# Ten more DMA transposes, issued from ScalarE's queue as well as SyncE's, with three smaller edits, in a fused linear-attention and MLP kernel

One Trainium2 chip, one core. The metric is device time in microseconds (us) of the core, median of several executions; lower is better. The kernel before takes 165.2 us. "Fast" and "slow" are two states in which executions of one kernel fall: a run that is over 1.5% longer than the fastest run of the same kernel is called slow, and only fast runs are compared.

## The reference

```python
def _attn_ref(q, k, v, alpha):                 # B, H, S, D = 4, 8, 768, 48, float32
    state = zeros((B, H, D, D))
    for t in range(S):
        state = alpha[:, :, t, :, None] * state + einsum('bhd,bhe->bhde', k[:, :, t], v[:, :, t])
        y[:, :, t] = einsum('bhd,bhde->bhe', q[:, :, t], state)
    return y

def _moe_ref(x, U, V, w_ch1, w_ch2):           # x: (4, 768, 384), the heads of y side by side
    h = x.transpose(0, 2, 1) @ U @ V           # U: (768, 32), V: (32, 768): low rank over time
    u = x + h.transpose(0, 2, 1)
    return u + maximum(u @ w_ch1, 0.0) @ w_ch2 # w_ch1: (384, 1536), w_ch2: (1536, 384)
```

The kernel cuts the 768 time steps of each of the four batches (0 to 3) into six chunks of 128. A chunk needs cumulated logarithms of alpha, k and q scaled by their exponentials (`rk`, `rq`), both transposed (`kt`, `qt`), scores, a causal mask (`pm`) and a running state (`st`). When a batch is complete, its x goes through the low-rank product (`utx`, then h), u = x + h, and two layers: MLP1 (`uT` times `w_ch1`, relu to `h1t`) and MLP2 (`h1t` times `w_ch2`, added to u). MLP1 needs u transposed: this is `uT`.

## The kernel before

The program calls `P.add` once for every operation; a long table then gives the order. A number in it is one `P.add`, and a letter behind it chooses the engine where there is a choice (A ScalarE, V VectorE, G GpSimd, S SyncE). Every engine works through its own operations in the order of the table. The table was made for this very program, so any edit of the operations needs a new one.

```python
PAIR = (0, 1)
TRD = {(3, c) for c in range(2, NC)}   # chunks whose k and q are transposed by DMA
TRU = (3,)                             # batches whose u is transposed by DMA
XT = (0, 1)                            # batches whose x is transposed, and h added in PSUM
# ... cut ...
# a chunk's decay totals: a zero or a large negative number (offd) is put under them by a
# matmul, then one activation
nc.tensor.matmul(cb()[:, DM : DM + 2 * HP], lhsT=ident, rhs=offd.rearrange("p a b -> p (a b)"), start=False, stop=False)
for p in range(HP):
    nc.tensor.matmul(cb()[:, DM + 2 * p : DM + 2 * p + 2], lhsT=lt()[:, 2 * p : 2 * p + 2, :].rearrange("t h w -> t (h w)"),
                     rhs=ones, start=False, stop=(p == HP - 1))
# ... cut ...
P.add({"ACT": 100}, lambda e: nc.scalar.activation(tot()[:, :, 0], cb()[:, DM : DM + 2 * HP], AF.Exp), r=[cb], w=[tot])
# ... cut: k and q of a chunk ...
if (b, c) in TRD:
    for ring, dst in ((rk, kT), (rq, qT)):
        P.add({"SP": 1250.0}, lambda e, ring=ring, dst=dst: nc.sync.dma_start(dst(), ring().rearrange("t h w -> t (h w)"), transpose=True),
              r=[ring], w=[dst], mode="X")
else:
    tk, tq = Buf(bank), Buf(bank)      # transposes on TensorE, then copies out of PSUM
# ... cut: u of a batch that is not in XT, chunk by chunk ...
P.add({"DVE": 465}, lambda e, c=c, hb=hb: nc.vector.tensor_tensor(ub()[:, c, :], xb()[:, c, :], hb()[:, 0:DM], op=ALU.add), ...)
if b in TRU:
    P.add({"SP": 1250.0}, lambda e, c=c: nc.sync.dma_start(uT()[:, :, c * C : (c + 1) * C], ub()[:, c, :], transpose=True),
          r=[(ub, c)], w=[(uT, c)], mode="X")
```

## Time and profile before

| | before |
|---|---|
| time, fast runs | 165.2 us (164.81 to 165.96) |
| span of the profiled run | 162.8 us |
| first MLP1 matmul | 29.4 us |
| end of the last matmul | 159.5 us |
| DMA transposes | 14, all issued by SyncE |

A profiled time in the views below is counted from the start of the span; the time of a run is some 2 us more than its span. The lines on which the reading rests stand in the prediction. To read a line of a group: source line, engine, operation, output and inputs, count, busy time and mean; in the chain of what ended last: start, length, what.

### The profile page before, as it was taken

How to read it: one execution, taken by the hardware profiler on the slowest of the kernel's cores; microseconds unless marked ns; L12 is line 12 of the kernel's file. 1: busy time of each engine (PE TensorE's matmuls, PEld its weight loads, DVE VectorE, ACT ScalarE, POOL GpSimd, SP SyncE). 2: the span in 40 equal slices, each digit the busy share in tenths (PEclk: the TensorE clock that was granted, in tenths of full speed). 3: DMA queues.
4: the chain of work that ended last, by engine and by line, in shares of the span. 5: the costliest groups of instructions: out<-in, count | busy, mean ns of one | idle time of the engine just before them, and what ended most of it. 6: DMA issues, size and time to landing. Idle time of an engine off the chain costs nothing.

```text
span 162.8 us, 4450 instructions
## 1 busy us (share of the span) xinstructions
PE 154.6 (95%) x1691; PEld 102.8 (63%) x1691; DVE 111.1 (68%) x240; ACT 87.9 (54%) x214; POOL 66.2 (41%) x106
## 2 busy tenths in 40 slices
PE   7878789999999999999999999999999999999991
PEld 2536677666666877766666766766667566666660
DVE  6389997536756989765579677896689465562512
ACT  4747787848594797956944557655432201330300
POOL 3228866659318625173685533519533000000000
PEclk9999999999999999999999999999999999999998
DMA  5999999999999999997998995995757133402124
GB/s 132 268 262 264 258 273 290 345 246 290 347 237 245 233 199 222 172 200 132 240 192 184 226 238 125 194 170 105 99 115 242 52 71 74 144 1 101 48 84 158
DMA packets 89876, 30.43 MB, mean 187 GB/s; under 512 B 83680, under 2 KB 89824, under 8 KB 89856
## 3 DMA queue, kind: packets, MB, share of 16 engines
q1 hardware_dynamic: 89856, 30.16, 81.7%
q8 instruction: 13, 0.21, 0.6%
q14 instruction: 7, 0.06, 0.1%
HBM read 23.79 MB, written 4.72 MB: 175 GB/s over the span
## 4 chain that ended last, share of the span: by engine, by line
PE 86%; DVE 6%; DMA 3%; SPq 2%; issue 1%
PE ps L798 29%; PE ps L773 29%; DMA io<-in_k_dram 3%; PE ps L435 3%; PE ps L543 2%; DVE pm L473 2%; SPq L356 2%; PE ps L604 2%; PE ps L625 2%; DVE rq L422 2%; PE ps L684 1%; PE ps L718 1%; PE ps L494 1%; PE ps L462 1%; PE ps L566 1%
## 5 line engine op out<-in xcount | busy, mean ns | idle before, releaser
L798 PE MATMUL ps<-w_sb,h1t 128*128 128x384 bf16 x288 | 54.2, 326 | 0.0
L773 PE MATMUL ps<-uT,w_sb 128*128 128x384 bf16 x288 | 50.9, 326 | 0.0
L783 ACT ACTIVATE h1t<-ps 128x384 bf16<-128x384 f32 x46 | 21.4, 496 | 35.4 <-PE ps L773 35.1
L785 DVE TENSOR_SCALAR h1t<-ps 128x384 bf16<-128x384 f32 x50 | 25.8, 552 | 21.0 <-PE ps L773 20.9
L773 PEld LDWEIGHTS <-w_sb 128*128 128x128 bf16 x288 | 27.3, 98 | 16.6
L798 PEld LDWEIGHTS <-h1t 128*128 128x128 bf16 x288 | 26.4, 97 | 16.4 <-issue 0.6
L635 DVE TENSOR_TENSOR pm<-ps,maskc 128x512 bf16<-128x512 f32 x24 | 15.6, 684 | 2.6 <-PE ps L625 2.5
L473 DVE TENSOR_TENSOR pm<-ps,maskp 128x512 bf16<-128x512 f32 x24 | 15.8, 682 | 1.3 <-PE ps L462 1.3
L584 POOL TENSOR_TENSOR rk<-io,ai 128x384 bf16<-128x384 f32 x12 | 11.0, 915 | 10.0 <-PE ps L773 3.9
L584 POOL TENSOR_TENSOR rq<-io,aa 128x384 bf16<-128x384 f32 x12 | 11.0, 927 | 2.2 <-ACT aa L578 1.2
L807 DVE TENSOR_TENSOR ou<-ub,ps 128x384 f32<-128x384 bf16 x12 | 6.4, 552 | 7.3 <-PE ps L798 7.1
L313 ACT CAST xb<-ps 128x384 bf16<-128x384 f32 x15 | 7.3, 491 | 7.0 <-PE ps L684 5.4
L317 POOL CAST rw<-io 64x384 bf16<-64x384 f32 x14 | 7.0, 503 | 8.0 <-DMA io<-in_v_dram 7.2
L317 POOL CAST rv<-io 128x384 bf16<-128x384 f32 x12 | 6.0, 503 | 9.6 <-DMA io<-in_v_dram 9.6
L317 POOL CAST w_sb<-io 128x384 bf16<-128x384 f32 x16 | 7.7, 507 | 4.7 <-DMA io<-in_moe_w_ch_dram 4.7
L313 ACT COPY kt<-ps 128x512 bf16<-128x512 bf16 x13 | 8.0, 612 | 2.5 <-PE ps L435 2.0
L313 ACT COPY qt<-ps 128x512 bf16<-128x512 bf16 x11 | 7.4, 677 | 3.3 <-PE ps L435 1.7
L315 DVE COPY qt<-ps 128x512 bf16<-128x512 bf16 x9 | 5.6, 627 | 4.6 <-PE ps L435 3.5
L659 POOL TENSOR_TENSOR st<-sm,tot 128x384 bf16<-128x384 f32 x6 | 5.0, 831 | 9.1 <-DVE sm L671 9.1
L422 POOL TENSOR_TENSOR rk<-io,ai 128x384 bf16<-128x384 f32 x8 | 7.3, 912 | 3.3 <-DMA io<-in_k_dram 1.4
L422 POOL TENSOR_TENSOR rq<-io,aa 128x384 bf16<-128x384 f32 x7 | 6.4, 913 | 5.3 <-ACT aa L416 5.3
L731 DVE TENSOR_TENSOR ub<-xb,ps 128x384 bf16<-128x384 bf16 x12 | 6.0, 550 | 3.3 <-PE ps L730 3.3
(120 smaller groups left out, 262.1 us busy)
## 6 DMA issues: line engine op xcount, KB each, us to landing
io<-in_q_dram SPq DMA_DIRECT2D x24, 192.0 KB, 4.4
...
```

What stands on the lines that cost most here:

```text
L313: nc.scalar.copy(dst, src)
L317: nc.gpsimd.tensor_copy(dst, src)
L422: eng.tensor_tensor(jh(dst()[:, :, 0:D]), raw(a), jh(x()), op=ALU.mult)
L473: nc.vector.tensor_tensor(dst, s2, maskp.to_broadcast([C, 2, 2, C]), op=ALU.mult)
L584: eng.tensor_tensor(dst()[:, :, 0:D], a(), x(), op=ALU.mult)
L635: nc.vector.tensor_tensor(pm()[:, :, par, :], s2, maskc.to_broadcast([C, HP, C]), op=ALU.mult)
L731: P.add({"DVE": 465}, lambda e, c=c, hb=hb: nc.vector.tensor_tensor(ub()[:, c, :], xb()[:, c, :], hb()[:, 0:DM], op=ALU.add), r=[hb] + xk( ...
L773: nc.tensor.matmul(hb()[:, 0:TW], lhsT=w1_sb[:, ct, jt * 128 : (jt + 1) * 128], rhs=uT()[:, ct, tt * TW : (tt + 1) * TW], start=(ct == 0), ...
L783: nc.scalar.activation(dst, hb()[:, 0:TW], AF.Relu)
L785: nc.vector.tensor_scalar_max(dst, hb()[:, 0:TW], 0.0)
L798: nc.tensor.matmul(hb()[:, 0:DM], lhsT=h1()[:, jt, c * C : (c + 1) * C], rhs=w2_sb[:, jt, :], start=(jt == 0), stop=(jt == NJ - 1 and not ...
L807: P.add({"DVE": 468}, lambda e: nc.vector.tensor_tensor(ou(), (xb if b in XT else ub)()[:, c, :], hb()[:, 0:DM], op=ALU.add), r=[hb] + (xk ...
```

## The change

The intent is to take work from TensorE, which is busy without a gap from 29.4 us on. The four parts, and the core of the diff (the order table is new as a whole and left out; `Plan.place`, which fits buffers to expected times, gets a case for transposes on ScalarE). A fifth part goes with the table: the diff also lets more operations choose their engine, and the new table uses it. Of the 24 scalings that make `rk` and `rq` of batches 2 and 3, all on GpSimd before, six now stand on VectorE, five of them for batch 3.

```diff
-    TRD = {(3, c) for c in range(2, NC)}
-    TRU = (3,)
-    XT = (0, 1)
+    TRD = {(3, c) for c in range(NC)}     # 4 more transposes of k and q by DMA
+    TRU = (2, 3)                          # 6 more transposes of u by DMA
+    XT = (0,)                             # batch 1's u as the sum x + h on VectorE
...
+    def queue(eng):
+        return nc.scalar if eng == "ACT" else nc.sync
...
-                    {"SP": 1250.0},
-                    lambda e, ring=ring, dst=dst: nc.sync.dma_start(dst(), ring().rearrange("t h w -> t (h w)"), transpose=True),
+                    {"ACT": 1250.0, "SP": 1250.0},
+                    lambda e, ring=ring, dst=dst: queue(e).dma_start(dst(), ring().rearrange("t h w -> t (h w)"), transpose=True),
... the same for the transpose of u ...
-            nc.tensor.matmul(cb()[:, DM : DM + 2 * HP], lhsT=ident, rhs=offd.rearrange("p a b -> p (a b)"), start=False, stop=False)
+        def f_tot(e):                     # the offset comes as the bias of two activations
+            for i in range(2):
+                nc.scalar.activation(tot()[:, i : 2 * HP : 2, 0], cb()[:, DM : DM + HP], AF.Exp, bias=offb[:, i : i + 1])
... MLP2: chunk 5 of batch 3 in two column parts, each with its add and its store ...
+        parts = [(0, 256), (256, DM)] if b == B - 1 and c == NC - 1 else [(0, DM)]
```

In the new table 19 of the 24 transposes are on ScalarE's queue and five on SyncE's (q of chunks 2 and 4 of batch 3; u1, u3 and u4 of batch 3). Where one queue's transposes follow the other's, the later ones must wait for the earlier ones to land.

More of the change, by code (lines that the diff above doesn't have):

```diff
@@ L118, in place @@
                 end[op] = dma + 850.0
+            elif eng == "ACT" and op.mode == "X":
+                dma = max(dma, t) + 500.0
+                clock[eng] = t + cost
+                end[op] = t + 2650.0
             elif eng == "SP":
@@ L153 @@
 TABLE = """
-67 65 69 179 61 182 201 184 157 77 62 63 183 66 204 160 205 187G 247 189 161 162 207 64 68 191V 164V 166 186V 188 190A 185 168V 165V 73 71 167 192 70
-181G 180G 224 206 163 159G 169V 81 74 170 194 172 193 75 158G 209G 3 78 79 76 82 72 195 250 227 196 208V 83 173 211 210 251 228 268 229 197 213A 2 231G
-171 174 80 271 175 198 212V 214 273 274 272 84 85 176 89 232V 233 253 252 234 215 254G 6 5 199 177 255G 4 226G 275G 203G 15 31 33 35 236V 23 13 17 93
-19 21 27 29 235A 237 43 25 87 86 1 97 39 90 216 200A 238 256 257 230 225A 259A 258V 240 202A 178A 241 239 242 260 277 276V 243 244 217 249G 218 270G
@@ L158 @@
-219 88 95 278 37 41 262 261 51 47 49 91 279A 245 220 280A 222 248A 94 269G 8 281 7 57 59 45 55 221 388 263 283 53 101 96 32 34 16 36 264 18 14 24 20 92
-284 285 98 105 391 410 394 246A 107 103 99 100 102 265 266 413 392 393 22 28 30 26 286 282 287 9 11 395G 0 267V 223V 288A 289 290 295 10V 12A 291A 414
-292 304 298 299 293 296 300A 396G 301 417G 302 305 297A 307 308 294V 306V 303V 309A 415 332 330 328 352 354 331A 329A 432 416 336 355V 353A 435 356 438
-357A 333V 344 312 340 320 314 345A 315A 313A 436 346 310 338 342 321V 455 337V 437 109 106 343V 112 104 108 113 316 398 334 318 347V 341V 335V 339V
@@ L162 @@
-311A 44A 40A 400A 390A 440G 38G 42G 348 458 397 419 326 322 317V 323V 349V 399A 327A 401 319A 461 389G 460 459 403 418V 421V 48G 439G 383 404 358 442
-324 325A 50A 402 405 406 368 46G 420 350 412G 52A 444A 58A 441 411G 434G 433G 462G 407G 351V 422V 443A 363 364 359 56A 54A 60A 478 423 445 384 369 370
-424 446 425 481 360 499 482 483 426 448 486G 447 361 371 449 502 385 365 505 450V 504 453 507G 427 386 428 366 509 464 488 485G 429G 511V 463V 110 362
-111 129 367 457A 503 456A 490A 454A 408 471 378 409A 619 466A 451 506V 465 430 487 508 117 379 133 467V 472 123 116 121 114 118 115 473G 468 119 120
@@ L166 @@
-122 489V 130 125 431A 484 510A 479A 480A 500A 131 127 124 387 136 474 135 126 128 137 149 491 512 470 452V 493 492 469 373 494 380 475G 501A 638 621
-374 495 640 515 623 622 496G 513 516 514 476 625 517V 375 497 627 381 629V 477A 626 620 642 641 376 718 498A 624 518 628 630V 720 519A 529 520 521 631
-722 721 723 658 522V 535 523 526 633 833 527 538 539 524 530 528A 525V 660 536 532 533 531A 537V 634 662 540A 661 663 545 561 551 635 534V 587 559 644
-664 645 639 585 588V 560A 581 546A 557 541 659 562A 643 569 567 632 553 570A 678 558A 542V 552V 554V 582A 372 134 666 575 680 145 573 681 682 574A 568A
@@ L170 @@
-683 586A 563 141 132 139 564A 668A 665 685 684 583 576V 584V 543 653 636 835 544A 646 837 647 547 555 649V 648A 637A 565 549 673 654 556V 548V 687 550A
-836 667 144 377 655G 679 674 686 589 571 590 688V 566V 669V 572V 725 675G 724 838 698 689A 690 650 670 671 651 652 699 591 700 579 702 703 701 852 580V
-592 692 705 704 609 656 594 595 727 693 577 691 657V 729A 672 694 578V 596 726 593 706 707 696 604 695V 597 697A 839 605 606 841 708A 709A 728A 713 714
-614 843A 138 730 710 732 712 872 890 676 610 840 719 715G 854 731 677V 711 611 612 607 857 855 599 733 842 892 856 908 734A 844A 834 858 859 874 716
@@ L174 @@
-615 717V 845 875 893 735 600 861 877 142 143 598 613 153 140 147 148 154 895 736A 894 150 146 876 863A 926 847 846 751 745 743 860 749 616 744 746 752
-853 878 750 739 740 848 601 879 753 747 737 850 849 617 862A 738 754A 864 151 155 867 928 741 851V 866 748A 783 910 781 782A 929 742V 784V 868 931 911
-773 797 865 602 880 798A 777 779 799 800A 912 913 785 765 930 786V 778V 780V 766V 870 757 932 891 896 871V 881 898 761 795 791 771 775 758A 772A 796V
-792V 787 873 897 915 933 914 869G 759 801 767 789 774A 768A 760A 776V 802V 885 899 917 763 769 788V 790V 886 916 887G 764A 770A 755 903 152 882 762V
@@ L178 @@
-909 900 918 756A 884 901 935 902 919 904 808 809 934 818 803 793 883 810 921 888 794A 156 905V 920 922 936 906 924 804 805 937 938 907A 923G 618 603
-608 382 927 939 940A 889V 925V 806 813 941 942A 828 946 807 958 819 943 949 947 950 959 829 955 820 814 952 948 815 823 824 944 825 956 951 945 953 826
-816 821 811 954 960 957 830 969 965 817 822 967 963 961 977 968A 966V 971 983 984A 964A 962V 981 972V 978V 985 1005 831 991 975 1014 973 976V 1009 970V
-987 1006A 992V 974A 986A 988V 982V 1010 979 980A 832 995 989 990V 996A 1011 1007 993 999 1015 1016 1001 997 1012 1002V 994V 1000V 1017 1019 1003 1034
@@ L182 @@
-1013 1020 812 1018 1021 1022 1029 1024 998A 1008A 1004A 1025 1026 1035 1030 1036 1027 1023 1028 827 1031 1037 1038 1032 1033
+61 73 69 62 68 63 224 157 160 227 163 161 201 162 65 1 164G 3 180G 4 165G 179 0 204 166 182 167 67 71 66 64 205 206 183 184 187V 169A 189 186G 77 70 81
+75 74 72 191V 188 78 168A 207 158G 159G 79 190V 209V 181A 228 185 230 76 82 170 192 195 173 247 229 208G 232G 171 194 231G 193 268 174 196 83 80 84 89
+250 211 85 6 210 172 5 212A 271 15 17 33 13 202G 234 175 197 176 198 213A 236A 251 214 233 199 216 203G 274 252 253 200A 272 254V 217 255G 218 256 258A
@@ new lines @@
+226A 273 225G 235V 275G 237 177 219 215 276G 220 257 240 238 221 239 27 25 29 86 31 241 21 19 259A 23 93 87 222 2 249G 242 269G 8 178A 277 260 7G 243
+223A 278 248A 245 279V 18G 280A 263 270A 410 264 281 261 262 265 244 282 388 266 16G 246A 14G 284 285 283 35 97 90 413 37 88 39 49 391 267A 286 43 94
+51 45 30G 28G 41 91 47 95 53 287 57 96 9 11 288A 289 12V 10A 290 298 292 295 301 22G 291A 392 293 299 296 300V 307 302 308 294A 92 99 59 304 297A 309A
+303A 305 306A 34A 26A 314 310 312 311A 336 338 313A 337A 348 322 350 334 349V 315V 339V 335V 323A 416 346 324 432 415 414 393 24G 20G 435 320 342 344
@@ new lines @@
+55 101 325A 347V 343V 345V 32G 396G 395G 389G 40G 36A 351A 321A 318 398 352 356 340 436 353A 438 397 319A 357V 399V 417V 341V 354 328 316 332 400A 329V
+419 355V 44G 439G 455 394 326 390A 38G 42G 418G 105 98 107 100 401 103 52A 437 421V 317V 403 402 404 441 333V 458 460 46A 461 50A 330 48G 363 443A 383
+368 364 420 58A 459 331A 405 406 440V 442 106 369 102 384 444A 434A 412G 407G 60A 56A 327V 422V 423 445 478 499 425 358 447 424 446 359 54G 411G 408
+426 409V 427 428 385 433G 463G 448 481 449 462V 450V 502 365 483 451 482 484 504 452V 386 507V 360 465 108 104 361 366 109 110 113 111 486G 453 370
@@ new lines @@
+467A 454A 503 367 112 129 362 117 488 430 114 121 131 118 116 485V 506V 464 487 509 508 371 466V 457A 431A 489A 511A 505 510V 490V 378 456G 429G 471
+119 122 120 133 115 123 130 125 468 512 472 480G 473G 479A 491 379 470 469 492 474 513 618 501A 500A 373 494 380 475G 515 495 476 620 493 516 496G 374
+514 497 517G 518 637 621 622 624G 477V 498V 623 519A 625V 375 619A 520 376 381 521A 627 626 633 629V 522 524 528 523 126 127 124 639 530 525 137 536
+628A 717 382 529 372 128 134 141 630 641 657 642 526 531 632 527A 640 532 534 135 659 719 533V 634 631 537 542 558 540 662 677 721 660 559A 552 679 535
@@ new lines @@
+553A 724G 643G 638A 722 538 554 645 541V 539V 647V 145 132 138 143 139 387 720 681 680 682 555A 661 562 563V 664G 683G 572 560 570 564 582 574 571V
+543V 561V 663G 568 566 652 583A 832 575A 565A 569A 834 584 666 685 653 573V 837 668A 835 836 658A 136 665 580 586 644G 684G 550 667A 687V 567V 581V
+585V 654G 686 149 150 144 377 140 672 646 548 551A 549A 673 674G 723G 678G 648V 635 688V 546 544 697 556 547V 587A 636A 545V 649 669 689 699 557V 700
+849 702 650 670 671 691 690 651 593 588 589 692 590 726 725 701 727V 591 693 703G 675 851 695 705 578 707V 728V 576 704G 706 694G 853 698A 579A 854 867
@@ new lines @@
+577A 852 696V 708V 838V 712 608 603 676V 713 729 709 840A 711 730 731 710 609 869 594 595 655 839G 841A 714G 718G 732 885 871 870 656A 715 872 733A 887
+610 596 855V 716V 734 874G 856G 735V 611 833G 592 146 151 612 155 147 153 842 604 142 154 148 745 605 598 857A 889 858A 888 890 843 746 844 850G 747A
+845 748 751 742 736 749 846 752 750A 753A 599 847 600 859 739 743 903 737 860 861 876S 613 614 615 865 862 905 848V 606 863 601 866V 740 784 792 778
+790 780 785V 781V 786 782 616 783V 793V 738A 907 906 800 798 788 796 909G 864G 779V 789V 868G 891G 892G 787V 910V 912S 152 744A 741A 766 776 768 607
@@ new lines @@
+156 791A 908 911A 762 921 894A 767V 873V 769V 801V 923 777A 925 924 886G 928G 760 772 763V 761V 794 754 880 756 926 893A 875A 795V 773V 774 881 882G
+930A 898 755V 797V 775V 899 927V 770 817 764 758 818 799A 771A 757V 759A 877 895 879 878 896 765A 897 913 802 929A 803 804 807 904G 900G 915 914 916
+901 917 918G 931 922G 933 932 919 808 827 883 934 597 935A 902A 809 828 920V 884V 936 937A 812 938 805 810 939 944 822 941 813 829 947 945 942 806 602
+617 943S 948 830 823 950 951 949S 952S 811 940A 946A 953 819 824 814 820 954 966 960 962 956 961A 967A 964 974 965V 957V 975V 825 970 968 958 972 955A
@@ L183 @@
+990 986 826 831 821 973V 969V 984 959V 987A 991A 994 1000 1002 963V 1003V 985V 1014 980 988 992 993V 1001V 981A 982 971A 983V 815 1009 1010 996 978 976
+979A 997V 977V 998 1015 999V 995A 1016 1004 1017 989V 1005 1006 1019 1020 1029 1021 1018 816 1007 1011 1008 1024 1022 1012 1032 1033 1030 1013 1025
+1023 1034 1026 1031 1027 1028
 """
@@ L254 @@
     ut_ones, upto, below = tri[:, 0, :], blocks[:, 0, :], blocks[:, 1, :]
-    ones = const.tile([C, 2], BF16, name="ones")
+    ones = const.tile([C, 1], BF16, name="ones")
     nc.vector.memset(ones, 1.0)
+    offb = const.tile([C, 2], FP32, name="offb")
+    nc.vector.memset(offb, 0.0)
+    nc.vector.memset(offb[0:64, 1:2], -30000.0)
+    nc.vector.memset(offb[64:128, 0:1], -30000.0)
     onesel = const.tile([C, 2, 2], BF16, name="onesel")
@@ L321, in small @@
         P.add({"SP": 500.0}, lambda e: nc.sync.dma_start(v_in, moe_V), w=["v_in"])
-        P.add({"POOL": 300}, lambda e: nc.gpsimd.tensor_copy(u_sb, u_in), r=["u_in"], w=["u"])
+        P.add({"POOL": 300, "ACT": 280}, lambda e: copy(e, u_sb, u_in), r=["u_in"], w=["u"])
         P.add({"POOL": 800}, lambda e: nc.gpsimd.tensor_copy(v_bf, v_in), r=["v_in"], w=["v_bf"])
@@ L341, in weights1 @@
             for ct in range(NCT):
-                weight(w1_sb[:, ct, cs], moe_w_ch1[ct * 128 : (ct + 1) * 128, cs], ("w1", g, ct), {"POOL": 485})
+                weight(w1_sb[:, ct, cs], moe_w_ch1[ct * 128 : (ct + 1) * 128, cs], ("w1", g, ct), {"POOL": 485, "ACT": 435})
     def weights2():
@@ L403, in f_cum @@
             nc.tensor.matmul(cb()[:, Q : 2 * Q], lhsT=upto, rhs=l2[:, 1], start=False, stop=False)
-            nc.tensor.matmul(cb()[:, DM : DM + 8], lhsT=ident, rhs=offd.rearrange("p a b -> p (a b)"), start=False, stop=False)
-            tot4 = cb()[:, DM : DM + 8].rearrange("p (c a b) -> p c a b", c=2, a=2)
+            nb = 2 if b == 0 else 1
+            if b == 0:
+                nc.tensor.matmul(cb()[:, DM : DM + 8], lhsT=ident, rhs=offd.rearrange("p a b -> p (a b)"), start=False, stop=False)
+            tot4 = cb()[:, DM : DM + 4 * nb].rearrange("p (c a b) -> p c a b", c=2, a=2)
             for a in range(2):
@@ L409, in f_cum @@
                         tot4[:, :, a, :], lhsT=lt()[:, HP * j + 2 * a : HP * j + 2 * a + 2, :].rearrange("t h w -> t (h w)"),
-                        rhs=onesel, start=False, stop=(a == 1 and j == 1),
+                        rhs=onesel[:, :, 0:nb], start=False, stop=(a == 1 and j == 1),
                     )
-        P.add({"PE": mm(DM, Q, Q, 8, 4, 4, 4, 4)}, f_cum, r=[lt], w=[cb])
+        P.add({"PE": mm(DM, Q, Q, 4, 4, 4, 4, *([8] if b == 0 else []))}, f_cum, r=[lt], w=[cb])
         aa, ai, tot = Buf(aas), Buf(ais), Buf(tots)
@@ L416, in stage_pair @@
         P.add({"ACT": 390}, lambda e: nc.scalar.activation(aa().rearrange("t h d -> t (h d)"), cb()[:, 0:DM], AF.Exp), r=[cb], w=[aa])
-        P.add({"ACT": 100}, lambda e: nc.scalar.activation(tot()[:, :, 0], cb()[:, DM : DM + 8], AF.Exp), r=[cb], w=[tot])
+        def f_tot(e):
+            if b == 0:
+                nc.scalar.activation(tot()[:, :, 0], cb()[:, DM : DM + 8], AF.Exp)
+                return
+            for i in range(2):
+                nc.scalar.activation(tot()[:, i : 2 * HP : 2, 0], cb()[:, DM : DM + HP], AF.Exp, bias=offb[:, i : i + 1])
+        P.add({"ACT": 100 if b == 0 else 200}, f_tot, r=[cb], w=[tot])
         rq, rk = Buf(rqs), Buf(rks)
@@ L560, in stage_gla @@
         rv = Buf(rvs)
-        P.add({"POOL": 480}, lambda e: copy(e, rv(), vt()), r=[vt], w=[rv])
+        P.add({"POOL": 480, "ACT": 420}, lambda e: copy(e, rv(), vt()), r=[vt], w=[rv])
         cb = Buf(bank)
@@ L566, in f_cum @@
             nc.tensor.matmul(cb()[:, 0:DM], lhsT=ut_ones, rhs=lt()[:, :, 0:D], start=True, stop=False)
-            nc.tensor.matmul(cb()[:, DM : DM + 2 * HP], lhsT=ident, rhs=offd.rearrange("p a b -> p (a b)"), start=False, stop=False)
             for p in range(HP):
                 nc.tensor.matmul(
-                    cb()[:, DM + 2 * p : DM + 2 * p + 2],
+                    cb()[:, DM + p : DM + p + 1],
                     lhsT=lt()[:, 2 * p : 2 * p + 2, :].rearrange("t h w -> t (h w)"),
@@ L573, in f_cum @@
                 )
-        P.add({"PE": mm(DM, 8, 2, 2, 2, 2)}, f_cum, r=[lt], w=[cb])
+        P.add({"PE": mm(DM, 1, 1, 1, 1)}, f_cum, r=[lt], w=[cb])
         aa, ai, tot = Buf(aas), Buf(ais), Buf(tots)
@@ L578, in stage_gla, with f_tot @@
         P.add({"ACT": 390}, lambda e: nc.scalar.activation(aa().rearrange("t h d -> t (h d)"), cb()[:, 0:DM], AF.Exp), r=[cb], w=[aa])
-        P.add({"ACT": 100}, lambda e: nc.scalar.activation(tot()[:, :, 0], cb()[:, DM : DM + 2 * HP], AF.Exp), r=[cb], w=[tot])
+        def f_tot(e):
+            for i in range(2):
+                nc.scalar.activation(tot()[:, i : 2 * HP : 2, 0], cb()[:, DM : DM + HP], AF.Exp, bias=offb[:, i : i + 1])
+        P.add({"ACT": 200}, f_tot, r=[cb], w=[tot])
         rq, rk = Buf(rqs), Buf(rks)
@@ L584, in f_scale @@
             eng.tensor_tensor(dst()[:, :, 0:D], a(), x(), op=ALU.mult)
-        both = {"POOL": 885}
+        both = {"POOL": 885, "DVE": 420}
         P.add(both, lambda e: f_scale(e, rk, kt, ai), r=[kt, ai], w=[rk], port=True)
@@ L733, in stage_mix @@
                 P.add(
-                    {"SP": 1250.0},
-                    lambda e, c=c: nc.sync.dma_start(uT()[:, :, c * C : (c + 1) * C], ub()[:, c, :], transpose=True),
+                    {"ACT": 1250.0, "SP": 1250.0},
+                    lambda e, c=c: queue(e).dma_start(uT()[:, :, c * C : (c + 1) * C], ub()[:, c, :], transpose=True),
                     r=[(ub, c)], w=[(uT, c)], mode="X",
@@ L789, in mlp2 @@
     def mlp2(b, xb, ub, utx, h1, c):
-        hb = Buf(bank)
         tt = c // NT
-        for g in range(3):
-            low = b in XT and g == 2
-            def f(e, g=g, low=low):
-                for jt in range(4 * g, 4 * g + 4):
-                    nc.tensor.matmul(
-                        hb()[:, 0:DM], lhsT=h1()[:, jt, c * C : (c + 1) * C], rhs=w2_sb[:, jt, :],
-                        start=(jt == 0), stop=(jt == NJ - 1 and not low),
-                    )
-                if low:
-                    nc.tensor.matmul(hb()[:, 0:DM], lhsT=vm_sb[:, c * C : (c + 1) * C], rhs=utx(), start=False, stop=True)
-            P.add({"PE": mm(*[DM] * (5 if low else 4))}, f, r=[(h1, tt, jt) for jt in range(4 * g, 4 * g + 4)] + [("w2", jt) for jt in range(4 * g, 4 * g + 4)] + ([utx] if low else []), w=[hb])
@@ L806, in mlp2, with f, f_o @@
-        ou = Buf(outs)
-        P.add({"DVE": 468}, lambda e: nc.vector.tensor_tensor(ou(), (xb if b in XT else ub)()[:, c, :], hb()[:, 0:DM], op=ALU.add), r=[hb] + (xk(b, xb, c) if b in XT else [(ub, c)]), w=[ou])
-        P.add({"SP": 550.0}, lambda e: nc.sync.dma_start(out[b, c * C : (c + 1) * C, :], ou()), r=[ou])
+        low = b in XT
+        base = xb if low else ub
+        ou = Buf(outs)
+        parts = [(0, 256), (256, DM)] if b == B - 1 and c == NC - 1 else [(0, DM)]
+        for n, (lo, hi) in enumerate(parts):
+            hb = Buf(bank)
+            groups = [range(NJ)] if len(parts) > 1 else [range(4 * g, 4 * g + 4) for g in range(3)]
+            for g, jts in enumerate(groups):
+                last = jts[-1] == NJ - 1
+                def f(e, jts=jts, hb=hb, lo=lo, hi=hi, last=last):
+                    for jt in jts:
+                        nc.tensor.matmul(
+                            hb()[:, 0 : hi - lo], lhsT=h1()[:, jt, c * C : (c + 1) * C], rhs=w2_sb[:, jt, lo:hi],
+                            start=(jt == 0), stop=(jt == NJ - 1 and not low),
+                        )
+                    if low and last:
+                        nc.tensor.matmul(hb()[:, 0 : hi - lo], lhsT=vm_sb[:, c * C : (c + 1) * C], rhs=utx()[:, lo:hi], start=False, stop=True)
+                need = [(h1, tt, jt) for jt in jts] + [("w2", jt) for jt in jts] + ([utx] if low and last else [])
+                cost = mm(*[hi - lo] * (len(jts) + (1 if low and last else 0)))
+                P.add({"PE": cost}, f, r=need, w=[hb])
+            def f_o(e, hb=hb, lo=lo, hi=hi):
+                nc.vector.tensor_tensor(ou()[:, lo:hi], base()[:, c, lo:hi], hb()[:, 0 : hi - lo], op=ALU.add)
+            P.add({"DVE": 70 + 398 * (hi - lo) // DM}, f_o, r=[hb] + (xk(b, xb, c) if low else [(ub, c)]), w=[(ou, n)])
+            P.add(
+                {"SP": 550.0 * (hi - lo) / DM + (0 if len(parts) == 1 else 60)},
+                lambda e, lo=lo, hi=hi: nc.sync.dma_start(out[b, c * C : (c + 1) * C, lo:hi], ou()[:, lo:hi]),
+                r=[(ou, n)],
+            )
```

## The prediction

> **What bounds the kernel now.** I read the page first: the busy shares and the forty slices.
>
> ```profile
> span 162.8 us, 4450 instructions
> ...
> PE 154.6 (95%) x1691; PEld 102.8 (63%) x1691; DVE 111.1 (68%) x240; ACT 87.9 (54%) x214; POOL 66.2 (41%) x106
> ...
> PE   7878789999999999999999999999999999999991
> ```
>
> TensorE is in front, VectorE has a third to spare, ScalarE half, and TensorE's gaps lie in the first six slices (to about 25 us). A busy PE may still be waiting in small pieces, so I checked the pace in the chain that ended last, in order of time, and in the table of stretches:
>
> ```profile
> 32.89 5.38 PE ps L773 x33
> ...
> 102.13 0.49 PE ps L730 x3
> ...
> 104.96 0.67 PE ps L746 x12
> ...
> 159.54 0.55 DVE ou L807
> ```
>
> A 384-column matmul costs 163 ns (5.38/33), a 128-column transpose 56 ns (0.67/12). From other rows of the chain: 83 ns for 192 columns, 42 for 96, about 27 for fewer than 64, and 0.1 us more when the array changes its tiling (a group of four MLP matmuls takes 0.65 us, 0.76 just after a tiled group). I decoded the order list: each number is one P.add in program order, 1,039 before and 1,035 after. All matmuls from the first MLP1 matmul on, at these paces, add up to 130.0 us. The trace has that first matmul at 29.4 and the last matmul's end at 159.5: 130.1 us. So **from 29.4 us on TensorE waits for practically nothing**, and every matmul removed there is gained, every new wait lost. Ahead lie 29.4 us of start (16.8 us of TensorE work, the rest filler and waits), behind lie 3.3 us of tail: the last add and its store.
>
> **What a DMA transpose costs**, from the rows of its two lines and the timeline:
>
> ```profile
> L735 SPq DMA_TRANSPOSE uT<-ub x6: 1186/1206/1248, 130.1 to 136.5; - x6
> ...
> DMA to landing us min/median/max: 2.3/2.4/2.4
> ```
>
> ```profile
> 130.06 7.68 SPq L735 DMA_TRANSPOSE uT<-ub  x6
> 130.09 0.49 PE L730 MATMUL ps<-utx,vm_sb 128*128 128x384 bf16 x2
> 130.26 0.58 PEld L798 LDWEIGHTS <-h1t 128*128 128x128 bf16 x4
> ...
> 135.94 6.50 PE L773 MATMUL ps<-uT,w_sb 128*128 128x384 bf16 x39
> ```
>
> Each holds its issuing queue for 1.2 us and lands 2.4 us after its issue began; on one queue they overlap, six in 7.7 us. The first three of this batch are u1, u2, u0, so MLP1 could start at 135.9 without a wait.
>
> **What the Trainium skill says.** (1) "DMA: Bandwidth & Descriptors", section "Silent corruption: two transposing streams in flight at once": transposes issued from SyncE and from ScalarE are two streams, in flight together they can corrupt each other, and the later stream's first transpose must wait for the earlier one's full completion count. The kernel before has one stream, so its trace says nothing on this. (2) Same page, section "Anatomy of one DMA": DMA engines do not wait on semaphores; the wait sits on the issuing sequencer. The trace agrees in so far as waits ahead of transposes stand on the SyncE queue (L735 waits 4.7 us in all for ub). (3) Same page, section "Issuing engines are not separate DMA queues": a second issuing engine saves only issue time; here that is 1.2 us each. (4) "TensorE: Matmul & The Clock Gate", "Part 4: PE-mode transpose": some 275 ns in a kernel's context, and a copy out of PSUM after it. The records do say 219 ns each, but the issue distance is 56 ns, and that is what counts in a dense stream.
>
> **The change, part by part.** TensorE first.
> - Ten more DMA transposes: four replace the k and q transposes of chunks 0 and 1 of batch 3 (16 x 56 ns = 0.9 us of PE and four evictions of about 0.6 us), six replace batch 2's u transposes (18 x 56 = 1.0 us and three evictions).
> - Batch 1's u as sums: the 18 accumulating transposes become 18 plain ones (nothing). Six low-rank matmuls into the transposed banks and six inside MLP2 go (12 x 163), six for h come (6 x 163): 1.0 us saved. VectorE gets six adds of 0.55, and six evictions of 0.5 become three of 0.55 to 0.8.
> - Totals: the matmul with offd goes from 18 of 24 chunks, 18 x 27 ns = 0.5 us less; 18 small activations come, 0.1 to 0.19 us each, 2 to 3 us of ScalarE, which has room.
> - Last MLP2 in two parts: 12 x (109 + 56) in place of 12 x 163 ns, nothing. In the new order list chunk 5 is not the last: the list ends with chunk 4, undivided, so the tail stays at 3.3 us.
> Sum on TensorE after the start: 0.9 + 1.0 + 1.0 + 0.5 = 3.4; recounted over the whole new list, with one more tiling change, 3.2 us. **Start:** the first load is now an alpha instead of a q (0.5 us earlier), VectorE has 31 instructions ahead of the first MLP1 instead of 40, GpSimd 30 instead of 37, ScalarE 54 instead of 49. VectorE was the packed one from 9 to 26 us, so I take 1.0 us, an estimate with 1 us of error either way. Without anything new: 165.2 - 3.2 - 1.0 = 161.0.
>
> **New waits.** Transposes in program order: seven on ScalarE (batch 3 chunks 0 and 1; u3, u4, u5 of batch 2), chunk 2's q on SyncE, u0 of batch 2 on ScalarE, chunk 4's q on SyncE, u2, u1 and six more on ScalarE, u1, u3, u4 of batch 3 on SyncE, u0, u2, u5 on ScalarE. Six changes of stream. I laid the new list out on TensorE's own paces, dense from 29.4. Batch 2's first MLP1 group that needs u0 to u2 is due at 109.6. If each change of stream waits for the other's landing: u3 to u5 issue from 99.6, the last at 102.0, lands 104.4; chunk 2's q 104.4 to 106.8; u0 to 109.2; chunk 4's q to 111.6; u2 at 111.6, u1 at 112.8, landed 115.2. TensorE's queue is in order: **5.6 us of wait.** In batch 3 the MLP1 is due at 132.8. u1, u3, u4 issue on SyncE at 129.3 to 131.9, the last lands at 134.3; u0 and u2 then issue on ScalarE at 134.3 and 135.5 and land at 137.9: **5.1 us of wait.** Without those waits u0, u2 (batch 3) would land at about 132.1 and u1 (batch 2) at about 109.9, just in time: the list was made for overlapping streams. Sum: 161.0 + 10.7 = 171.7, rounded to 171.5.
>
> **Rivals.** (a) No such waits, or the streams' order does not bite: 161 to 162. For it: the list's due times fit overlapping streams to within 0.5 us, and somebody found the list worth keeping. Against: the skill's rule; a program without the waits would risk wrong data. (b) One of the two places waits only, say because batch 2's chain starts earlier than I walked it: 166. (c) VectorE becomes the bound: from batch 1's to batch 3's U product it has 106 instructions instead of 86, 62 us at their recorded lengths, 53 at their back-to-back pace (four adds of 0.55 took 1.95), against 61.5 us of TensorE. Full at 87%, it could add 1 to 3 us of scattered waits to (a), making 162 to 164. (d) ScalarE holds 19 issues of 1.2 us, 23 us, in a stretch where it was at most 63% busy in any 5 us; evictions queued behind them hold PSUM banks. In the main case this hides inside the same waits.
>
> **Range and chances.** Stream waits in both places (about six in ten): 169 to 174.5. One place or partial: one in eight, 163 to 168. None: under three in ten, 160.5 to 163.5, and 2% is 161.9 there, so most but not all of it counts as faster. The range takes in all but the edges: 161 to 174.5. Chances: faster 0.26, within 2% 0.15, slower 0.59.
>
> **What would show it.** TensorE gaps of 4 to 6 us just ahead of batch 2's MLP1 on u0 to u2 (near 109) and batch 3's (near 132), released by a DMA of uT; on the queues, SyncE's transposes waiting for ScalarE's landings and the reverse; the first MLP1 matmul at about 28.4; 1,691 matmuls less 16 + 18 + 6 + 18, plus 12, so 1,645 (fillers aside). I am wrong if the transposes of the two queues overlap in time, or if the gaps are small because the walk above has the chain too late; and the start is wrong if the first MLP1 matmul is not before 29.4.

## The result

The kernel after takes **174.81 us** (median of four; fast runs 174.98, 174.65, 173.31, with a mean of 174.3; one slow run of 177.44) against 165.0 for the kernel before in the same session. The ratio is 1.056, 95% interval 1.047 to 1.065. Here and below a ratio is the mean time of one kernel's fast runs over that of the other's fast runs of the same rounds, so it is not quite the ratio of the medians quoted.

The page of the kernel after, its first lines, the slices of TensorE and of its clock, and the queue that carries the transposes:

```profile
span 173.0 us, 4395 instructions
...
PE 156.5 (90%) x1649; PEld 101.7 (59%) x1649; DVE 118.9 (69%) x263; ACT 84.8 (49%) x217; POOL 61.2 (35%) x98
...
PE   7989999999999999999999988798199987599991
PEclk9999999999999999999999999999759999999999
...
q10 hardware_dynamic: 9184, 2.20, 8.3%
```

There are 42 fewer matmuls. The unbroken row of nines of before has holes in its last third, one slice down to 1 (about 121 to 125 us), and the clock falls to 5 tenths just after it. What TensorE waited for (engine, line, tile, releaser: us in total, times, longest):

```profile
PE ps L799 <- DMA uT<-ub: 5.2, 4, 1.9
PE ps L651 <- DMA kt<-rk: 4.4, 1, 4.4
...
PE ps L651 <- DVE ub L757: 0.5, 1, 0.5
```

The same view of the kernel before has no wait for a transpose, and none over 0.8 us after the start-up filler:

```profile
PE ps L306 <- DVE filler L244: 1.2, 1, 1.2
PE ps L435 <- DVE rq L422: 1.1, 3, 0.7
```

The chain that ended last, in order of time (start, length), in the kernel after:

```profile
106.84 5.17 DMA uT<-ub
...
116.73 2.43 DMA qt<-rq
119.25 1.35 ACTq L621
120.70 4.19 DMA kt<-rk
124.93 1.46 PE ps L651 x24
126.39 4.34 PE ps L829 x16
...
141.21 2.53 DMA uT<-ub
...
147.89 2.75 DMA uT<-ub
```

A q transpose of SyncE lands at 119.2, ScalarE issues its next two at once behind it, the second lands at 124.9, and only then do the scores of batch 3 (line 651) run. The late landing seems in part a consequence of the wait: two loads of v and two stores that stood behind SyncE's waiting transposes went out at 118.0 to 119.7, beside ScalarE's next two k, which took 5.4 and 4.2 us to land. In the profile of experiment 9, where SyncE did not wait for ScalarE, these loads went at 115.1 and 116.9, and the same two k landed in 2.4 and 2.5 us. The timeline of the two queues around it, first SyncE's, then ScalarE's:

```profile
115.33 2.60 SPq L621 DMA_TRANSPOSE qt<-rq  x2
...
141.21 3.78 SPq L761 DMA_TRANSPOSE uT<-ub  x3
```

```profile
110.82 1.21 ACTq L621 DMA_TRANSPOSE qt<-rq  x1
119.25 2.70 ACTq L621 DMA_TRANSPOSE kt<-rk  x2
...
137.40 2.52 ACTq L761 DMA_TRANSPOSE uT<-ub  x2
147.89 1.20 ACTq L761 DMA_TRANSPOSE uT<-ub  x1
```

No two of these overlap across the queues. ScalarE's first twelve go as one stream up to 110.8; SyncE's two q wait 4.9 us for their landing and go at 115.3; ScalarE resumes at 119.25 and goes on to 125.6; later u is passed from ScalarE to SyncE (141.2) and back (147.9). The transposes of u, with SyncE's longest semaphore wait (4,896 ns) and the landing times:

```profile
L761 ACTq DMA_TRANSPOSE uT<-ub x9: 1193/1220/2394, 98.5 to 147.9; - x9
...
L761 SPq EVENT_SEMAPHORE  x3: 17/28/4896, 136.2 to 142.5; - x3
...
DMA to landing us min/median/max: 2.3/3.4/5.5
```

The landing of u took 2.3 to 2.4 us in the kernel before, here up to 5.5; that of k and q here has a median of 4.2 us:

```profile
DMA to landing us min/median/max: 2.4/4.2/5.4
```

The table of stretches (after the stretch: its length, the busy time of TensorE, its weight loads, VectorE, ScalarE and GpSimd with their instruction counts, granted clock, DMA share, GB/s):

```profile
120.00:125.00 5.00, 0.61 (x6) 0.17 (x5) 0.29 (x1) 1.64 (x4) 1.29 (x2) 0.79 0.97 211
125.00:130.00 5.00, 5.00 (x37) 2.90 (x38) 3.68 (x6) 0.00 (x0) 0.00 (x0) 0.53 0.33 30
...
140.00:145.00 5.00, 3.27 (x21) 1.79 (x19) 1.83 (x4) 0.00 (x0) 0.00 (x0) 1.00 0.28 62
145.00:150.00 5.00, 3.91 (x25) 2.16 (x22) 3.00 (x7) 0.87 (x2) 0.00 (x0) 1.00 0.41 119
```

After the gap TensorE runs at a clock of 0.53: 16 matmuls of MLP2 take 4.34 us, 271 ns each where the prediction read 163 ns.

Where the 10.2 us of span went, by the prediction's own sum:

| term | predicted | in the trace |
|---|---|---|
| TensorE's work from the first MLP1 on, its matmuls counted at undisturbed paces | -3.2 us | 130.0 to 126.8 us: -3.2 |
| start | -1.0 | 29.4 to 27.9 us: -1.5 |
| tail | 0 | 3.3 to 3.6 us: +0.2 |
| waits of TensorE | +10.7 | 0.5 + 0.55 + 1.0 + 4.4 + 1.74 + 1.86 = +10.1 |
| slow clock after the longest wait | none | about +2.4 |
| not traced to a wait, remainder | none | about +2.3 |

The start is read in TensorE's timeline:

```profile
27.91 5.53 PE L799 MATMUL ps<-uT,w_sb 128*128 128x384 bf16 x33
```

The 2.4 us are 4.34 less 16 x 0.163 = 1.7, and 1.46 us for 24 score matmuls at about twice their usual pace = 0.7. Summed, -3.2 - 1.5 + 0.2 + 10.1 + 2.4 + 2.3 = +10.3. The distances between the starts of matmuls settle most of the remainder. A wait in the view is counted from the end of the matmul before it; in a dense stretch the next one would have started 0.16 us earlier, which is 1.0 us for six waits. About 1.4 us more are pauses of under 0.4 us each, most of them between 33 and 97 us, which before has not.

Of the 10.1 us of waits only 4.4, 1.74 and 1.86, together 8.0, stand behind a change of stream. The 0.55 and 1.0 ahead of and in batch 2's MLP1 are waits for ScalarE's own transposes that landed late, and the 0.5 is a wait for VectorE.

The start is one draw of a thing that varies: with the same table and the same start the first MLP1 stands at 27.9, 28.6 and 28.8 us in the other fast profiles (experiments 6, 1 and 5), and in the kernels with the old totals at 28.9 to 29.4 (before and experiments 3, 4 and 8).

### The profile page after: what moved, and what is told of

Read it like the earlier page. It is cut to its first block, busy times and chain, and to the rows that moved or that the text cites. A ratio compares the mean times of both kernels' runs of the same rounds, so it can differ in the third digit from the quotient of the medians.

```text
span 173.0 us, 4395 instructions
## 1 busy us (share of the span) xinstructions
PE 156.5 (90%) x1649; PEld 101.7 (59%) x1649; DVE 118.9 (69%) x263; ACT 84.8 (49%) x217; POOL 61.2 (35%) x98
## 4 chain that ended last, share of the span: by engine, by line
PE 61%; DMA 18%; DVE 7%; ACT 5%; SPq 3%; issue 2%; ACTq 1%; POOL 1%; DVEq 0%; POOLq 0%
PE ps L829 23%; PE ps L799 19%; DMA uT<-ub 8%; DMA io<-in_alpha_dram 4%; SPq L368 3%; DMA kt<-rk 2%; DMA io<-in_k_dram 2%; PE ps L457 2%; PE ps L651 2%; PE ps L630 2%; PE ps L484 2%; PE ps L565 2%; PE ps L516 2%; DMA qt<-rq 1%; DVE rk L610 1%
## 5 line engine op out<-in xcount | busy, mean ns | idle before, releaser
L829 PE MATMUL ps<-w_sb,h1t 128*128 128x384 bf16 (+2 forms) x300 | 54.4, 326 | 0.0
L811 DVE TENSOR_SCALAR h1t<-ps 128x384 bf16<-128x384 f32 x60 | 30.6, 552 | 19.0 <-PE ps L799 19.0
L829 PEld LDWEIGHTS <-h1t 128*128 128x128 bf16 x300 | 27.9, 99 | 17.1 <-issue 2.2
L809 ACT ACTIVATE h1t<-ps 128x384 bf16<-128x384 f32 x36 | 16.5, 498 | 35.2 <-PE ps L799 24.3
L841 DVE TENSOR_TENSOR ou<-ub,ps 128x384 f32<-128x384 bf16 (+2 forms) x19 | 9.9, 528 | 6.0 <-PE ps L829 5.8
L322 ACT CAST xb<-ps 128x384 bf16<-128x384 f32 x14 | 6.5, 489 | 10.2 <-PE ps L710 9.2
L757 DVE TENSOR_TENSOR ub<-xb,ps 128x384 bf16<-128x384 bf16 x18 | 9.3, 549 | 2.6 <-PE ps L756 2.6
L581 ACT ACTIVATE lt<-io 128x384 bf16<-128x384 f32 x12 | 6.3, 521 | 7.2 <-DVE pm L661 3.9
L610 POOL TENSOR_TENSOR rk<-io,ai 128x384 bf16<-128x384 f32 x8 | 7.3, 912 | 5.2 <-ACT ai L598 5.2
L651 PE MATMUL ps<-qt,kt 48*128 48x128 bf16 x96 | 4.6, 240 | 4.9 <-DMA kt<-rk 4.4
L599 ACT ACTIVATE aa<-ps 128x384 bf16<-128x384 f32 x12 | 6.0, 496 | 6.0 <-PE ps L590 4.7
L444 POOL TENSOR_TENSOR rk<-io,ai 128x384 bf16<-128x384 f32 x7 | 6.8, 966 | 5.1 <-ACT ai L429 4.4
L326 POOL CAST rv<-io 128x384 bf16<-128x384 f32 x8 | 4.0, 502 | 12.5 <-DMA io<-in_v_dram 12.5
```

The lines of the kernel that those rows point to most:

```text
L326: nc.gpsimd.tensor_copy(dst, src)
L444: eng.tensor_tensor(jh(dst()[:, :, 0:D]), raw(a), jh(x()), op=ALU.mult)
L610: eng.tensor_tensor(dst()[:, :, 0:D], a(), x(), op=ALU.mult)
L651: nc.tensor.matmul(sc[par]()[:, p * C : (p + 1) * C], lhsT=kT()[o : o + D, p, :], rhs=qT()[o : o + D, p, :], start=(p == 0), stop=(p == HP ...
L809: nc.scalar.activation(dst, hb()[:, 0:TW], AF.Relu)
L811: nc.vector.tensor_scalar_max(dst, hb()[:, 0:TW], 0.0)
```

## The experiments

Twelve kernels ran. The theory is: *the changes of stream cost the time*. Rivals: ScalarE's queue, whose 19 issues stand ahead of evictions; the order in one queue; VectorE's load. No run puts the six scalings of the fifth part back on GpSimd, so their share is untested. "Table" means the order table. An experiment whose table I adapted by hand is called so: its result contains whatever that table loses.

### 1 and 2: one queue for all transposes (after's table otherwise)

```diff
-876S ... 912S ... 943S ... 949S 952S         # e1: A in place of S, five tokens
+876A ... 912A ... 943A ... 949A 952A         # e2: S on all 24
```

> The changed kernel with its five SyncE transposes put on ScalarE's queue too; nothing else differs. Stream theory (a change of queue makes the later transposes wait for the landing of the earlier queue's): no queue changes are left, so the 4.4 us gap ahead of batch 3's scores, the cold clock after it and the two gaps of batch 3's MLP1 go: 162 to 166 us, against 174.8. Contention theory (transposes land late, 3.4 to 5.5 us, because loads share the DMA engines): gaps stay, 171 us or more. ScalarE theory (issues of 1.2 us on ScalarE's queue hold up its evictions): no better or worse, 173 to 177.

> The changed kernel with all 24 transposes on SyncE's queue. Stream theory: also one stream, so most of the loss goes, but SyncE issues in order with the loads and stores of the same time, so 163 to 169 us. Contention theory: no change, 171 or more. ScalarE theory: clearly better than with all on ScalarE.

Measured: all on ScalarE 181.34 us (ratio 1.096, 1.091 to 1.100), all on SyncE 185.39 (1.121, 1.117 to 1.125). With no change of stream left both are slower than the kernel after, so my expectation failed outright. The chain of the first shows why:

```profile
112.18 0.48 DVE rq L610
...
112.68 1.21 ACTq L621
...
113.93 1.29 ACTq L761
...
115.26 3.55 DMA uT<-ub
```

A queue issues in its own order. In after's table the q transpose of chunk 4 stands ahead of u2 and u1; on SyncE it stood in another queue than they, but in the one queue u2 and u1 now wait until VectorE has made chunk 4's `rq` (112.18), one of the six scalings moved from GpSimd, which itself stands on VectorE behind the relus of MLP1's first half. TensorE waits 7.3 us there, and 4.3 us more in a second place, batch 3's MLP1:

```profile
PE ps L799 <- DMA uT<-ub: 11.6, 2, 7.3
```

On SyncE the same `rq` blocks the queue for 7.5 us, with the loads behind it. (That run's profile is of a slow execution; its time above is of fast ones.) The two runs therefore say little about streams. They show that a table made for two queues may not be folded into one.

### 3: the kernel before, its 14 transposes on ScalarE's queue

```diff
-  {"SP": 1250.0}, ... nc.sync.dma_start(..., transpose=True)
+  {"SP": 1250.0, "ACT": 1250.0}, ... queue(e).dma_start(..., transpose=True)   # table: A on all 14
```

> The kernel before with its 14 transposes on ScalarE's queue in place of SyncE's. Stream theory: one stream still, so within 1% of before, 164 to 167 us. ScalarE theory: 14 issues of 1.2 us in ScalarE's order cost something that can be seen: 168 us or more.

Measured: 168.95 us, ratio 1.022 (1.018 to 1.026). One stream, no change, same table, and 3.9 us slower. So the rival that ScalarE's issues cost something is confirmed, by a wait of TensorE that the kernel before has not (scores behind an eviction by ScalarE, which stood behind transposes):

```profile
PE ps L633 <- ACT h1t L791: 2.3, 1, 2.3
```

The chain shows the eviction between two issues, and what came after:

```profile
120.29 1.16 ACTq L603
...
121.50 0.49 ACT h1t L791
121.99 0.38 ACTq L603
122.37 0.39 ACT h1t L791
122.76 0.46 PE ps L633 x8
123.22 4.25 PE ps L806 x16
```

The 16 MLP2 matmuls behind the wait take 4.25 us, 1.6 us more than at 163 ns each: the clock fell, to 0.50 in the stretch from 124 to 126 us. The wait and the slow clock together make the 3.9 us.

### 4: the kernel before, batch 3's u split between the queues

```diff
-u0..u5 of batch 3 on SyncE
+u2, u3, u4 of batch 3 on ScalarE, u0, u1, u5 on SyncE    # table: A on three tokens
```

> The kernel before with batch 3's six u transposes divided between the queues (u2, u3, u4 on ScalarE, the other three on SyncE): three changes of queue and nothing else. Stream theory: each change costs one landing of 2.4 us in the series; MLP1 of batch 3 starts about 1.4 us late and its second half 0.4 us late: 166.5 to 168 us. Contention and ScalarE theories: same as before, 165 us.

Measured: 166.89 us, ratio 1.011 (1.007 to 1.016), 1.9 us over the kernel before. The queues alternate, and the issues come in this order: SyncE 129.7, ScalarE 132.1, SyncE 134.6, ScalarE 138.4. Each start comes 2.4 to 2.6 us after the other queue's last issue, where the landing took 2.3 to 2.4. This is the mechanism in a place without loads, on a table whose order was not touched: the six that took 7.7 us on one queue take over 11 us on two. TensorE's waits in the trace:

```profile
PE ps L781 <- DVE ou L815: 1.2, 1, 1.2
...
PE ps L781 <- ACT h1t L791: 0.5, 1, 0.5
```

```profile
132.08 8.80 ACTq L743 DMA_TRANSPOSE uT<-ub  x3
```

The first ends at 136.94, 0.09 us after u0 has landed (136.85), so I read it as a wait for the transpose, though the view names a VectorE add. The second is not a wait for u at all: relus of ScalarE stand behind its transposes, which wait for SyncE's landings. So even here ScalarE's queue has a part in the loss.

### 5: after, all on ScalarE, the table mended

u2, u0 and u1 of batch 2 are moved ahead of the k and q of batch 3, and batch 3's u into the order in which VectorE makes it (hand-adapted).

```diff
+moved: u2 u0 u1 of batch 2 ahead of k, q of chunks 2 to 4 of batch 3; u0..u5 of batch 3 behind their adds; all with A
```

> All 24 transposes on ScalarE's queue as in the run that took 181 us, but the order list mended: batch 2's u2, u0, u1 stand ahead of the q and k of batch 3 whose sources come later, and batch 3's u in the order in which the sums are made. Head-of-line theory (a transpose whose source is late holds everything behind it in the queue): the 9 us gap ahead of batch 2's MLP1 and the cold clock after it go, 163 to 169 us. Contention theory (transposes land in 4 to 5.5 us beside loads, whatever their order): 171 or more. If the queue's own 1.2 us per issue in front of evictions is the main cost: 169 to 173.

Measured: 170.71 us, ratio 1.033 (1.028 to 1.039). This is 10.6 us better than the folded table of experiment 1, so the blocked queue was most of that one's loss. By the means of the fast runs it is 3.8 us better than after, but not below 169, as I had expected if the order were the whole matter; it falls in the band that I had given for a cost of ScalarE's queue itself. TensorE waits in five places for 0.4 to 1.8 us each, two of them behind a ScalarE eviction and three for transposes; the largest three groups:

```profile
PE ps L799 <- DMA uT<-ub: 2.0, 2, 1.6
PE ps L674 <- ACT h1t L809: 1.8, 1, 1.8
PE ps L651 <- DMA qt<-rq: 1.7, 1, 1.7
```

Its clock stays full throughout.

### 6: after, the ten added transposes back on TensorE

```diff
-    TRD = {(3, c) for c in range(NC)}
-    TRU = (2, 3)
+    TRD = {(3, c) for c in range(2, NC)}
+    TRU = (3,)                            # 14 transposes, all on SyncE; the table adapted by hand
```

> The changed kernel with one part undone: the ten added DMA transposes are PE transposes again, and the 14 others stand on SyncE's queue; the order list is else the changed one, the other three parts stay. If the added transposes and their queues are the whole loss: 161.5 to 165 us. If the new order list or the fuller VectorE have their own loss: 166 to 170.

Measured: 171.47 us, ratio 1.038 (1.032 to 1.044): above both bands. No stream waits remain, yet TensorE waits 3.0 us for a `kt` whose source, again a scaling moved to VectorE, stands late there between relus, and the clock falls to 0.66 after it. The table was made for transposes that leave TensorE and VectorE free, so this is not a clean undoing. It shows only that the other parts under this table do not give 161 us by themselves.

### 7: before, with the biased exponentials alone

```diff
+    nc.scalar.activation(tot()[:, i : 2 * HP : 2, 0], cb()[:, DM : DM + HP], AF.Exp, bias=offb[:, i : i + 1])   # in place of the offd matmul, 18 chunks
```

> The kernel before with one part of the change: totals by two biased exponentials in 18 chunks, the offd matmul gone there. TensorE's sum is 0.5 us less, ScalarE's 2 to 3.5 us more, off the path: 164.2 to 165.2 us.

Measured: 163.58 us, ratio 0.990 (0.987 to 0.993): 1.5 us gained, below the band (0.5 was predicted), and on an unchanged table. In the profiled run the gain is not where the prediction put it. From the first MLP1 matmul (28.47 us) to the last matmul's end TensorE takes 130.1 us, as before; the first MLP1 comes 0.9 us earlier. That recurs: three kernels with this edit start it at 28.4 to 28.5 us (7, 10 and 11), four without at 28.9 to 29.4 (before, 3, 4 and 8). Why the start gains is not settled.

### 8: before, with the last MLP2 in two parts

In the table of before the list ends with chunk 4 as well, so I divided chunk 4, the one that is last.

```diff
+        parts = [(0, 256), (256, DM)] if b == B - 1 and c == NC - 2 else [(0, DM)]
```

> The kernel before with the division into 256 and 128 columns applied to the chunk whose MLP2 is last in its order list (chunk 4). The last add is of 128 columns (about 0.25 us in place of 0.55) and the last store of 64 KB (1.5 us to landing in place of 2.2): 0.5 to 1.0 us less, 164.0 to 164.6 us.

Measured: 164.46 us, ratio 0.995 (0.992 to 0.998), as expected; the table got the divided chunk's new entries. The last add takes 0.29 us on 128 columns where it took 0.55 on 384. In after the division is on chunk 5, and the last add is still of 384 columns (0.56 us).

### 9: after, SyncE's five transposes as plain copies

With this, table, queues and dependencies stay, but only ScalarE transposes, so nothing waits for the other stream. Its output is wrong, which doesn't matter for the time.

```diff
-  queue(e).dma_start(..., transpose=True)
+  nc.scalar.dma_start(..., transpose=True) if e == "ACT" else nc.sync.dma_start(<same tiles, not transposed>)
```

> Wrong on purpose. The changed kernel with the same order list and the same queues, but the five transfers on SyncE's queue are plain copies of the same bytes, so only one queue transposes and no transfer waits for the other queue's landing. Stream theory (changes of queue are most of the loss): the gap of 4.4 us ahead of batch 3's scores, the cold clock after it and the two gaps in batch 3's MLP1 go or shrink to under 1 us, 8 to 10 us less: 163 to 167.5 us. Theory that the ten added transfers cost it by landing late and by holding ScalarE's queue: 170 us or more, as in the single-queue runs (170.7).

Measured: 167.85 us (fast runs 168.83, 166.86, 166.47; the profiled run, 170.12, is slow), ratio 1.014 (1.007 to 1.022). This is the upper edge of the band for the theory and below the rival's. The mean of the fast runs is 167.4 against 174.3 for after: **the waits between the streams, with what follows from them, cost 6.9 us** (some 5 to 9 by the two intervals). What follows are the slow clock, the loads that SyncE held back and the late landings beside them. The longest wait, and the stretches where after had its gaps:

```profile
PE ps L799 <- DMA uT<-ub: 2.4, 1, 2.4
```

```profile
120.00:125.00 5.00, 5.00 (x39) 3.13 (x37) 4.58 (x10) 1.85 (x6) 2.48 (x4) 1.00 0.41 88
...
140.00:145.00 5.00, 5.00 (x33) 3.02 (x31) 2.28 (x6) 0.87 (x2) 0.00 (x0) 1.00 0.41 103
145.00:150.00 5.00, 5.00 (x33) 2.99 (x32) 3.41 (x7) 0.88 (x3) 0.00 (x0) 1.00 0.32 118
```

The gap ahead of the scores, the slow clock behind it and both gaps in batch 3's MLP1 are gone. Two waits for transposes are left: 0.9 us for a q, and u1 of batch 2, issued at 109.8, takes 5.9 us to land, beside loads (DMA share over 1 in that stretch), and TensorE waits 2.4 us, with the clock at 0.66 after it.

### 10: before, with parts 7 and 8 together

> The kernel before with the totals of the change and the last MLP2 in two column parts, on the chunk that is last in its list. If the two gains (1.5 and 0.6 us alone) add: 162.7 to 163.4 us.

```diff
+edits of experiments 7 and 8 in one kernel
```

Measured: 163.55 us, ratio 0.991 (0.988 to 0.993). This is 1.5 us faster than before, but by its time no better than experiment 7 alone, against my expectation. The profiled spans do differ by the tail, 161.4 against 161.8 us; a gain of 0.4 to 0.6 us is about what the intervals of the two runs leave open, so whether the gains add is not shown.

### 11: experiment 10, with batch 1's u as sums

```diff
-    XT = (0, 1)
+    XT = (0,)                             # table adapted by hand around batch 1's low-rank product
```

> As the run before, and batch 1's u as sums (the third part of the change; a hand-made place in the list). TensorE has 1.0 us less; if the chain U product, sums, transposes, evictions is covered by the matmuls put beside it, 161.7 to 163.0 us; if not, 163.5 to 165.

Measured: 167.31 us, ratio 1.013 (1.011 to 1.016): missed. In the stretches from 60 to 75 us TensorE is busy 3.88, 4.40 and 3.62 of 5 us each, where the kernel before has 5.00 in each. My hand-made order puts the sums and the transposes behind one another there. So this part's gain of 1.0 us on TensorE is neither shown nor refuted.

### 12: experiment 5, batch 3's u on SyncE

One change of stream, in a place where the earlier stream landed long before.

```diff
-940A ... 946A 942 943A ... 949A ... 952A ... 955A
+940S ... 946S 942 943S ... 949S ... 952S ... 955S
```

> The mended list (all transposes on ScalarE's queue, 170.7 us), now with the last batch's six u transposes on SyncE: one change of stream, in a slack place: ScalarE's last transpose of that kernel issued at 124.9 us and was down before 129, the first u is ready at 135.7. If a change costs only where its landing is awaited (my theory): no wait of SyncE's queue for a landing, 169.5 to 171.2 us. If every change of stream costs about its 2 us wherever it stands: 172.5 to 173.5. If ScalarE's six issues (7.2 us of its queue) were themselves what holds that kernel above 165: 167 to 169.

Measured: 174.27 us, ratio 1.053 (1.047 to 1.058; fast runs 173.0 to 174.7, the profiled one slow). The time is above all three bands. The change itself cost nothing that the trace shows: SyncE waited for ScalarE's landings while it had nothing else to issue, and what released its first u, at 138.8, was VectorE's add. But SyncE also carries the stores. Its timeline, then TensorE's:

```profile
138.82 3.87 SPq L761 DMA_TRANSPOSE uT<-ub  x3
142.74 3.19 SPq L846 DMA_DIRECT2D out_dram<-ou  x3
145.98 3.26 SPq L761 DMA_TRANSPOSE uT<-ub  x2
```

```profile
147.62 2.88 PE L799 MATMUL ps<-uT,w_sb 128*128 128x384 bf16 x11 [2.63 <-DVE ou L841]
```

Three stores stand behind three transposes; the first goes at 142.7 and is down at 146.9, only then is an output tile free for VectorE's next add, and TensorE waits 2.6 us behind that add. So the theory "a change costs only where its landing is awaited" holds in the trace and yet missed the time. I had left out the neighbours in the queue. As the profile is of a slow run, I don't split the 3.6 us over experiment 5 further.

## Why the prediction came true where it did

**The direction and the mechanism were right.** The changes of stream are real waits in the trace, no two streams overlap, and taking them away alone brings 6.9 us (experiment 9). The rival that there are no such waits (161 to 162 us) is refuted. The fast runs' mean of 174.3 stands at the upper end of the stated range; the point, 171.5, was short by 2.8 us.

**TensorE's saved work was right:** 3.2 us, as the trace's matmuls give at their paces. The matmul count was right too: 1,649, which is the 1,645 and four more fillers (19 where before has 15). **The start** gave 1.5 instead of 1.0 us, within its scatter. The undivided tail was read correctly from the list.

**The waits came out at the right sum in the wrong places.** The step that laid the list out in program order failed. I counted six changes, the trace has four, because ScalarE's first twelve transposes went as one stream; why the built program orders them so the runs do not show. Ahead of batch 2's MLP1, where 5.6 us were predicted for changes of stream, none stood, and TensorE lost 0.55 + 1.0 to late landings. The large wait, 4.4 us, was two changes in series ahead of batch 3's scores, for the k of chunk 2, issued behind the k of chunk 3, which I had not followed at all because I looked at u only. In batch 3's MLP1 5.1 us were predicted in one place, and 1.74 + 1.86 came in two. That the sums agree, 10.7 and 10.1, is luck: only 8.0 us of the 10.1 stand behind a change of stream, and the largest of them at a place that the prediction did not have.

**Landings of 2.4 us** were taken from six transposes in a stretch almost without loads. Beside loads they took up to 5.5 us in after and 5.9 in experiment 9. In after this makes the 106.84 landing 5.17 us, and it is the longest wait left in experiment 9.

**The clock was missing from the sum.** The Trainium skill, "TensorE: Matmul & The Clock Gate", section "Why this matters for your kernels", says to leave no gap over some 3 us between bursts of matmuls, since a window of idleness takes the clock back to half. After the 4.4 us gap the trace shows 0.53, worth about 2.4 us; in the kernel after, gaps up to 1.9 us left it at full. Gaps of the section's length and less were enough here, in fast runs: 3.0 us in experiment 6 (0.66 in the stretch after it) and 2.3 us in experiment 3 (0.50). Such a wait must therefore be counted with a surcharge, 1.6 us in experiment 3.

**Rival (d), ScalarE's issues, is real, and I said that it would hide inside the other waits.** On the kernel before it costs 3.9 us with the slow clock behind it (experiment 3). In experiment 5 it is one of the waits that keep a kernel without any change of stream at 170.7. In after itself TensorE waits for a ScalarE eviction for 0.2 us at most, so there it did hide. **Rival (c), a full VectorE,** was seen only through the order: relus ahead of the moved scalings, `rq` in experiment 1 and `rk` in experiment 6.

**What stays open.** Without any waits, after's span would be 27.9 + 126.8 + 3.6 = 158.3 us, a time of about 160. With the streams' waits gone it was 167.4. In that experiment's profile, of a slow run, stand the wait for the late landing, the slow clock behind it, two waits of 0.9 to 1.0 us (for a q and for an `rk` on VectorE) and a first MLP1 1.4 us later than in after, but none behind a ScalarE eviction; the runs do not divide the seven us between. Nor do they show whether the ten transposes could gain at all with a table made for one queue.

## What to carry to other kernels

Before moving transposes to a second queue, draw the transposes of both queues on one time axis, add one landing for every change of queue, at the landing time measured beside the loads of that place, and follow every consumer and not the best-known one. Then look at what stands behind each issue in its queue, whether evictions on ScalarE or stores and loads on SyncE: an in-order queue passes every wait on, which with its slow clock cost 3.9 us in experiment 3, without any change of stream. Here the small edit that left the order alone (totals by a bias) gained 1%, and no version with more or moved transposes gained anything.

## What the Trainium skill lacked or had wrong

- "DMA: Bandwidth & Descriptors", section "Silent corruption: two transposing streams in flight at once", gives the rule but no price. The runs show 1.9 us for three changes of queue in a place without loads, each start 2.4 to 2.6 us after the other queue's last issue (experiment 4; 0.5 us of it by relus held in ScalarE's queue), and 6.9 us for four changes in after, slow clock included (experiment 9). In experiment 12 a change whose earlier stream had landed long before was followed by no wait for it.
- The same page, section "Issuing engines are not separate DMA queues", treats the issuing engine as a matter of an issue time that is usually small beside the transfer. A transpose's issue held its queue for 1.2 us of the 2.4 us to its landing, and moving 14 issues from SyncE to ScalarE cost 3.9 us of 165 (experiment 3), through an eviction that stood behind them and the slow clock after it.
- No page that I read has the landing time of a DMA transpose beside other traffic: 2.3 to 2.6 us alone, up to 5.5 us (after) and 5.9 us (experiment 9) while loads kept the DMA engines busy.
- "TensorE: Matmul & The Clock Gate", "Part 4: PE-mode transpose", gives some 275 ns in a kernel's context, a duration, and no distance between two in a dense stream. Here the record is 219 ns long, but such a transpose takes 56 ns of TensorE's time, so that sending 34 of them to the DMA engines freed only 1.9 us.
- The same page, section "Why this matters for your kernels": after a gap of 4.4 us the clock was 0.53, and after gaps of up to 1.9 us full, which agrees. But the section's figure of about 3 us is not a safe limit: in a fast run the clock fell to 0.50 after a gap of 2.3 us (experiment 3).
